# Half sums of the activations at other places in VectorE's order, one of them moved from GpSimd to VectorE

## The chip, the cores and the metric

The kernel runs on one core of a Trainium2 chip. The metric is the device time of one execution in microseconds (us); of several executions the median is given. TensorE does the matrix products, VectorE and ScalarE read their results out of the score banks (PSUM) and work on them, GpSimd takes a share of the elementwise work and issues part of the transfers, and DMA queues move data. An engine executes its instructions in the order of its own queue; engines wait for each other by semaphores.

## The reference

Eight batches of eight heads of attention over 576 positions with 64 features, each head with one of two masks, and then two linear layers with a leaky activation:

```
scores = where(mask, q @ k.T / 8, -1e9)         # heads 0-3: the last 32 positions; heads 4-7: every 32nd
attn   = softmax(scores)
x      = (attn @ v), heads side by side          # 4608 tokens x 512
h      = x @ w_in                                # 512 -> 2048
g      = max(h, 0) + alpha * min(h, 0)
out    = g @ w_out                               # 2048 -> 512
```

## The kernel before

The 4608 tokens are nine chunks of 512 (n = 0 to 8). For each chunk the outer loop runs through positions i. At i = 0 to 15, layer 1 (`lin1_piece`, L608 to L619) makes one 128-row piece of h each: four TensorE products into a bank `hps`, ScalarE's `neg` from the bank (L616), and, one step later, VectorE's `gT` from `neg` and the bank (L619). The bank is free when that `gT` is done; there are three such banks. In chunks 2 to 8 the order of the pieces puts the even ones of each half ahead of the odd ones.

Layer 2 of chunks 2 to 8 (`lin2_fast`, L733 and L743) forms its product from seven block products instead of eight, which takes sums of blocks of g and of w_out. g is cut into token halves t and interleaved feature halves j, g(t, j), and the four sums (here S0 to S3, in the code `gsum[0..3]`, made by `g_sum`, L677) are

- S0 = g(1,0) + g(1,1)
- S1 = S0 - g(0,0)
- S2 = g(0,0) - g(1,0)
- S3 = g(0,1) - S1

Each sum is made in two halves h: half 0 from pieces 0 to 7 (made at i = 0 to 7), half 1 from pieces 8 to 15. A table `sums` says after which position i which half of which sum is made, and on which engine. At i = 16 and 17, TensorE multiplies g(0,0); at 18 it takes S0's half 0 and at 19 S0's half 1 (L733); at 20 and 21 S1's halves; at 22 and 23 g(0,1); at 24 and 25 S2; at 26 and 27 S3; at 28 and 29 g(1,1). The first S0 product takes the bank that the last `gT` has freed.

Between these positions stand the steps of attention for later batches (`attn_n`), in chunks 1 to 6: a head pair's scores on TensorE (L376, banks `sp` and `sph`), their exponentials on ScalarE (L399, L405), the product with a mask on GpSimd (L401, L408), the product with v on TensorE (L429, bank `pv`), and the normalization on VectorE: the reciprocal of the row sum (L436) and the product with it (L438, into `x` or `x16s`). `pv`, `sph` and the transposes `tp` and `xp` share three banks (`pspool`) in turn, so a later one waits until the normalization of an earlier one has read its bank. A strided pair has three such normalizations in a row (`x16s`).

Nothing reorders the instructions: each engine has them in the order in which the loop emits them. At the end of position i the loop first runs the attention steps due there, and then the half sums that the table lists for i.

Of the kernel before, what the change touches and what calls it, by code (L numbers as in the profile page):

```python
# [32 lines left out]
def kernel(  # L33
# [540 lines left out]
    def attn_until(b):  # L574

        return max(i for i, (g, _) in enumerate(pieces) if g == 4 * b + 3) + 1
# [3 lines left out]
    def attn_step(end):  # L580
        while late:
            late.pop(0)()
        if pos["i"] < end:
            pieces[pos["i"]][1]()
            pos["i"] += 1
        if defer:
            defer.pop(0)()
        while after:
            after.pop(0)()
# [6 lines left out]
    def lin1_piece(n, m, begin=False):  # L596
        if n not in gTs:
            gTs[n] = gpool.tile([128, 16, 512], F16, tag="gT", name="gT")
        c0 = (512 * n) % RING
        hps = begun.pop(m, None)  # L600
        if hps is None:
            pool, tag = (pspool, "ps") if n == 0 and m // 3 % 2 else (phpool, "hps")
            hps = pool.tile([128, 512], F32, tag=tag, name="hps")
            order = (2, 3, 0, 1)
        else:
            order = (0, 1)
        for kk in order[0:2] if begin else order:
            keep(nc.tensor.matmul(  # L608
                hps, win16[:, kk, 128 * m : 128 * m + 128], xT[:, kk, c0 : c0 + 512],
                start=(kk == 2), stop=(kk == 1)))  # L610
        if begin:
            begun[m] = hps
            return

        neg = npool.tile([128, 512], F32, tag="neg", name="neg")
        keep(nc.scalar.activation(neg, hps, AF.Relu, scale=-1.0))  # L616

        def fin():
            keep(nc.vector.scalar_tensor_tensor(  # L619
                gTs[n][:, m, :], neg, oma[:, m : m + 1], hps, op0=ALU.mult, op1=ALU.add))  # L620
        late.append(fin)
# [3 lines left out]
    def lin2_piece(n, i):  # L625
        mt, part = i // 4, i % 4
        last = n == NCH - 1
        if part == 0:
            ops_cur["t"] = phpool.tile([128, 512], F32, tag="hps", name="ops")
        ops = ops_cur["t"]  # L630
        r0 = 512 * n + 128 * mt
        if last and mt == 3:

            if part in (1, 3):
                return
            c0 = 128 * part
            half = phpool.tile([128, 512], F32, tag="hps", name="ops3") if part else ops
            for kf in range(16):
                keep(nc.tensor.matmul(
                    half[:, 0:256], gTs[n][:, kf, 128 * mt : 128 * mt + 128],  # L640
                    wout16[:, kf, c0 : c0 + 256], start=(kf == 0), stop=(kf == 15)))
            osb = opool.tile([128, 512], F32, tag="osb", name="osb")
            keep(nc.vector.tensor_copy(osb[:, 0:256], half[:, 0:256]))
            keep(nc.sync.dma_start(out[r0 : r0 + 128, c0 : c0 + 256], osb[:, 0:256]))
            return
        for kf in range(4 * part, 4 * part + 4):
            keep(nc.tensor.matmul(  # L647
                ops, gTs[n][:, kf, 128 * mt : 128 * mt + 128], wout16[:, kf, :],
                start=(kf == 0), stop=(kf == 15)))
        if part == 3:  # L650
            osb = opool.tile([128, 512], F32, tag="osb", name="osb")
            keep(nc.scalar.copy(osb, ops))
            keep(nc.sync.dma_start(out[r0 : r0 + 128, :], osb))


    def wout_sum(i):

        def w(j, c):
            return wout16.rearrange("p (i j) c -> p i j c", j=2)[:, :, j, 256 * c : 256 * c + 256]

        o, a, b = (
            (0, w(0, 1), w(0, 0)), (1, w(1, 1), wsum[0]),
            (2, w(1, 1), w(0, 1)), (3, w(1, 0), wsum[1]))[i]
        keep(nc.vector.tensor_tensor(wsum[o], a, b, op=ALU.subtract))

    def g_sum(n, i, h, eng="dve"):

        gv = gTs[n].rearrange("p (i j) c -> p i j c", j=2)
        hs = slice(4 * h, 4 * h + 4)

        def g(t, j):
            return gv[:, hs, j, 256 * t : 256 * t + 256]

        a, b, op = (
            (g(1, 0), g(1, 1), ALU.add), (gsum[0][:, hs], g(0, 0), ALU.subtract),
            (g(0, 0), g(1, 0), ALU.subtract), (g(0, 1), gsum[1][:, hs], ALU.subtract))[i]
        keep((nc.vector if eng == "dve" else nc.gpsimd).tensor_tensor(gsum[i][:, hs], a, b, op=op))  # L677
# [149 lines left out]
    def attn_n(n, end):  # L827
        for _ in range(n):
            attn_step(end)
        if n == 0:  # L830
            attn_step(0)
# [108 lines left out]
    for pr in range(2):  # L940
# [5 lines left out]

    FAST = 2
    sums = {
        5: [(2, 0, "pool")], 9: [(0, 0, "pool")], 15: [(0, 1, "dve"), (1, 0, "dve")],
        16: [(1, 1, "dve")], 18: [(2, 1, "dve")], 19: [(3, 0, "dve")], 20: [(3, 1, "dve")]}  # L950

    for n in range(1, NCH):
        ab = attn_until(n + 1) if n + 1 < B else len(pieces)
        left = ab - pos["i"]
        acc = -1.5 if n == 1 else 0.0
        for i in range(32 if n < FAST else 30):
            if i < 16:
                lin1_piece(n, i if n < FAST else 8 * (i // 8) + 2 * (i % 4) + i % 8 // 4)
            elif n < FAST:
                lin2_piece(n, i - 16)  # L960
            else:
                lin2_fast(n, i - 16)
            acc += left / (22 if n < FAST else 19.5 if n == B - 2 else 21) * (0.5 if i < 16 else 1.0)
            cnt = int(acc)
            acc -= cnt
            attn_n(cnt, ab)
            if n < FAST:
                if i in (18, 21, 24, 27):
                    wout_sum((i - 18) // 3)
                continue  # L970
            for z, h, eng in sums.get(i, ()):
                g_sum(n, z, h, eng)
        while pos["i"] < ab:
            attn_step(ab)
# [30 lines left out]
```

## Time and profile before

| what | value |
|---|---|
| median of 3 runs | 299.87 us (299.77 to 300.31) |
| profiled execution, time | 300.08 us |
| profiled execution, span of the core | 298.3 us |
| half sums on VectorE (L677) | 42, shortest 0.675 us, longest 1.767 us |
| half sums on GpSimd (L677) | 14, median 2.122 us |
| start of layer 1, chunk by chunk, 3 to 8 | 122.74, 153.05, 183.36, 213.67, 242.69, 268.74 us |

A profile is of one execution. In the rows of a timeline the first number is the start in us from the span's start, the second the length in us, then engine, line, operation, the tiles (written <- read), the shapes, the count of merged instructions, and in brackets the idle time before them with what ended it. "PE" is TensorE, "DVE" VectorE, "ACT" ScalarE, "POOL" GpSimd.

### The profile page before, as it was taken

To read this page: it belongs to the slowest core of one execution; us is meant where nothing else is said; L and a number is where in the kernel's file an instruction comes from. 1 tells how busy PE (TensorE), PEld (TensorE's weight loads), DVE (VectorE), ACT (ScalarE), POOL (GpSimd) and SP (SyncE) were. 2 spreads that over 40 slices of the span, in tenths; PEclk is the share of its full clock that TensorE was granted. 3 is DMA by queue.
4 is the path that set the end of the run, shared out by engine and by line. 5 is a ranking of instruction groups with operands and counts; after the bars stand their busy time and mean duration, and the time that the engine had idled before them with its cause. 6 is when DMAs were issued, how large, how long until landed. Compare 5 with 4: busy or idle time off the path is not lost.

```text
span 298.3 us, 6835 instructions
## 1 busy us (share of the span) xinstructions
PE 292.3 (98%) x2684; PEld 182.7 (61%) x2684; DVE 219.1 (73%) x406; ACT 178.5 (60%) x332; POOL 175.5 (59%) x164
## 2 busy tenths in 40 slices
PE   8999999999999999999999999999999999999995
PEld 3764555544554477646864687468745974784484
DVE  5688876668775897588848984898489948926852
ACT  1777755697557774776477646764676356516730
POOL 8462571059869998979897988495553405002300
PEclk9999999999999999999999999999999999999999
DMA  7999999999998969999999999967711140022004
GB/s 183 256 194 201 242 206 260 206 185 321 126 193 144 115 100 102 206 156 139 123 154 180 156 138 177 174 98 79 211 22 21 20 144 2 0 73 70 0 2 142
DMA packets 96976, 41.18 MB, mean 138 GB/s; under 512 B 75360, under 2 KB 93232, under 8 KB 96944
## 3 DMA queue, kind: packets, MB, share of 16 engines
q0 software_dynamic: 51008, 17.77, 60.8%
q1 hardware_dynamic: 45584, 22.32, 34.7%
q10 hardware_dynamic: 352, 0.66, 0.9%
q8 instruction: 21, 0.34, 0.5%
q14 instruction: 11, 0.09, 0.1%
HBM read 38.24 MB, written 9.44 MB: 160 GB/s over the span
## 4 chain that ended last, share of the span: by engine, by line
PE 80%; DVE 8%; ACT 4%; DMA 3%; issue 3%; SPq 1%; POOL 0%; DVEq 0%; ACTq 0%
PE hps L608 38%; PE ops L743 18%; PE ops L647 5%; PE ops L733 5%; PE pv L429 4%; DMA ql<-in_q_dram 3%; DVE gsum L677 2%; PE ops L908 2%; PE sp L376 2%; DVE gT L619 2%; DVE x16s L438 1%; ACT neg L616 1%; PE sph L376 1%; PE xp L454 1%; DVE x L438 1%
## 5 line engine op out<-in xcount | busy, mean ns | idle before, releaser
L608 PE MATMUL hps<-xT,win 128*128 128x512 f16 x576 | 132.2, 379 | 0.0
L619 DVE SCALAR_TENSOR_TENSOR gT<-neg,oma,hps 128x512 f16<-128x512 f32 x144 | 105.3, 744 | 36.0 <-ACT neg L616 28.1
L616 ACT ACTIVATE neg<-hps 128x512 f32<-128x512 f32 x144 | 85.8, 597 | 34.6 <-PE hps L608 32.5
L608 PEld LDWEIGHTS <-win 128*128 128x128 f16 x576 | 53.5, 98 | 58.6 <-issue 0.2
L677 POOL TENSOR_TENSOR gsum<-gT 128x1024 f16<-128x1024 f16 x14 | 29.7, 2123 | 41.7 <-DVE gT L619 36.7
L401 POOL TENSOR_TENSOR et<-et,consts 128x576 f16<-128x576 f16 (+1 forms) x24 | 35.5, 1477 | 28.0 <-ACT et L399 27.9
L743 PEld LDWEIGHTS <-gT 128*128 128x128 f16 x336 | 31.4, 98 | 5.4 <-issue 0.3
L438 DVE TENSOR_TENSOR x<-pv,rc 96x384 f16<-96x384 f32 (+2 forms) x62 | 33.0, 532 | 2.1
L408 POOL TENSOR_TENSOR et<-et,consts 128x576 f16<-128x576 f16 (+1 forms) x24 | 31.5, 1311 | 0.0
L429 PEld LDWEIGHTS <-et 72*128 72x128 f16 (+1 forms) x448 | 23.4, 98 | 11.4 <-DVE x L438 0.8
L743 PE MATMUL ops<-wout,gT 128*128 128x256 f16 x224 | 27.9, 273 | 0.1
L733 PE MATMUL ops<-wsum,gsum 128*128 128x256 f16 x216 | 26.6, 273 | 0.0
L399 ACT ACTIVATE et<-sp 128x576 f16<-128x576 f32 (+1 forms) x24 | 15.5, 644 | 17.1 <-PE sp L376 17.1
L234 POOL COPY vs<-stv 72x1024 f16<-72x1024 f16 x14 | 15.3, 1104 | 16.5 <-DMA stv<-in_v_dram 16.5
L743 PEld LDWEIGHTS <-gsum 128*128 128x128 f16 x224 | 20.8, 98 | 2.6
L733 PEld LDWEIGHTS <-gsum 128*128 128x128 f16 x224 | 20.8, 97 | 2.7
L436 DVE RECIPROCAL rc<-pv 96x6 f32<-96x6 f32 (+2 forms) x80 | 14.6, 183 | 10.2 <-PE pv L429 10.1
L688 DVE TENSOR_TENSOR osb<-ops,par 128x512 f32<-128x512 f32 (+1 forms) x14 | 9.4, 673 | 15.7 <-PE ops L743 8.2
L405 ACT ACTIVATE et<-sph 128x288 f16<-128x288 f32 (+1 forms) x48 | 18.8, 409 | 0.0
L686 ACT COPY osb<-ops 128x512 f32<-128x512 f32 x14 | 8.2, 586 | 16.8 <-PE ops L743 16.7
L647 PE MATMUL ops<-wout,gT 128*128 128x512 f16 x64 | 16.4, 380 | 0.0
L760 ACT COPY par<-ops 128x512 f32<-128x512 f32 x13 | 7.6, 585 | 14.0 <-PE ops L733 14.0
(111 smaller groups left out, 363.4 us busy)
## 6 DMA issues: line engine op xcount, KB each, us to landing
out_dram<-osb SPq DMA_DIRECT2D x35, 256.0 KB, 4.0
vl<-in_v_dram POOLq DMA_DIRECT2D x6, 384.0 KB, 8.6
win<-in_moe_w_in_dram POOLq DMA_DIRECT2D x4, 512.0 KB, 17.9
wout<-in_moe_w_out_dram POOLq DMA_DIRECT2D x4, 512.0 KB, 16.8
qsd<-in_q_dram POOLq DMA_DIRECT2D x7, 288.0 KB, 6.9
ksd<-in_k_dram POOLq DMA_DIRECT2D x7, 288.0 KB, 7.9
stv<-in_v_dram POOLq DMA_DIRECT2D x7, 288.0 KB, 7.3
ql<-in_q_dram SPq DMA_DIRECT2D x3, 576.0 KB, 7.6
```

The source lines that it names most:

```text
L401: keep(nc.gpsimd.tensor_tensor(mv, mv, m, op=ALU.mult))
L405: keep(nc.scalar.activation(ev[:, n * y : n * y + n], sps[y][0:r, 0:n], AF.Exp, scale=SCALE))
L408: keep(nc.gpsimd.tensor_tensor(mv, mv, m, op=ALU.mult))
L429: keep(nc.tensor.matmul(pv[:, 65 * x : 65 * x + 65], et[0:r, c : c + 128], v16[0:r, 2 * P.pr + hh, t, :] if P.strided else v16[:, 6 * (2 * ...
L438: keep(nc.vector.tensor_tensor(P.x16[0:w, c0 : c0 + 64 * nb].rearrange("r (c e) -> r c e", e=64), pvv[:, :, 0:64], rc[0:w, 0:nb].unsqueeze ...
L608: keep(nc.tensor.matmul(hps, win16[:, kk, 128 * m : 128 * m + 128], xT[:, kk, c0 : c0 + 512], start=(kk == 2), stop=(kk == 1)))
L616: keep(nc.scalar.activation(neg, hps, AF.Relu, scale=-1.0))
L619: keep(nc.vector.scalar_tensor_tensor(gTs[n][:, m, :], neg, oma[:, m : m + 1], hps, op0=ALU.mult, op1=ALU.add))
L647: keep(nc.tensor.matmul(ops, gTs[n][:, kf, 128 * mt : 128 * mt + 128], wout16[:, kf, :], start=(kf == 0), stop=(kf == 15)))
L677: keep((nc.vector if eng == "dve" else nc.gpsimd).tensor_tensor(gsum[i][:, hs], a, b, op=op))
L733: keep(nc.tensor.matmul(o, gsum[i][:, y, 128 * z : 128 * z + 128], wsum[i][:, y, :], start=(x == "5" and y == 0 and (z == 0 or alone)), st ...
L743: keep(nc.tensor.matmul(o, lhs(y), rhs(y), start=(first and y == 0), stop=(y == 7), skip_group_check=True))
```

## The change

The table of half sums is replaced by two, one for chunk 2 (`FAST`) and one for chunks 3 to 8. In chunks 3 to 8, S1 half 0 is made at i = 13 instead of 15, S1 half 1 at 17 instead of 16, S2 half 1 at 19 instead of 18, and S3 half 0 at 20 instead of 19. In chunk 2, S0 half 0 is made by VectorE at i = 12 instead of by GpSimd at i = 9, S1 half 0 stays at 15, and the rest is as in the other table. The work of every half sum is the same.

```diff
     FAST = 2
     sums = {
-        5: [(2, 0, "pool")], 9: [(0, 0, "pool")], 15: [(0, 1, "dve"), (1, 0, "dve")],
-        16: [(1, 1, "dve")], 18: [(2, 1, "dve")], 19: [(3, 0, "dve")], 20: [(3, 1, "dve")]}
+        5: [(2, 0, "pool")], 9: [(0, 0, "pool")], 13: [(1, 0, "dve")], 15: [(0, 1, "dve")],
+        17: [(1, 1, "dve")], 19: [(2, 1, "dve")], 20: [(3, 0, "dve"), (3, 1, "dve")]}
+    sums2 = {
+        5: [(2, 0, "pool")], 12: [(0, 0, "dve")], 15: [(0, 1, "dve"), (1, 0, "dve")],
+        17: [(1, 1, "dve")], 19: [(2, 1, "dve")], 20: [(3, 0, "dve"), (3, 1, "dve")]}
...
-            for z, h, eng in sums.get(i, ()):
+            for z, h, eng in (sums2 if n == FAST else sums).get(i, ()):
                 g_sum(n, z, h, eng)
```

An entry `i: [(z, h, engine)]` reads: after position i, half h of sum Sz on that engine.

## The prediction

> **What bounds the kernel now.** First the page: TensorE is busy 98% of the span at the full granted clock, so only time that TensorE itself loses can be won back.
>
> ```profile
> PE 292.3 (98%) x2684; PEld 182.7 (61%) x2684; DVE 219.1 (73%) x406; ACT 178.5 (60%) x332; POOL 175.5 (59%) x164
> ...
> PEclk9999999999999999999999999999999999999999
> ```
>
> Busy time hides short waits, since a matmul's recorded length covers its successor's start. So I read TensorE's timeline from start to start where the change works: chunk 3 (its second layer starts at 138.07), with chunks 4 and 5 repeating it 30.31 us and 60.62 us later, and chunk 2.
>
> ```profile
> 143.03 0.30 PE L376 MATMUL sp<-qT,kT 64*128 64x96 f16 x6
> 143.16 0.56 PE L376 MATMUL sph<-qT,kT 64*128 64x96 f16 x6
> 143.65 1.05 PE L733 MATMUL ops<-wsum,gsum 128*128 128x256 f16 x8
> 144.66 0.34 PE L429 MATMUL pv<-vs,et 72*128 72x65 f16 x6
> ...
> 149.61 0.30 PE L376 MATMUL sp<-qT,kT 64*128 64x96 f16 x6
> 149.75 0.29 PE L376 MATMUL sph<-qT,kT 64*128 64x96 f16 x6
> 149.97 1.05 PE L743 MATMUL ops<-wout,gsum 128*128 128x256 f16 x8
> 150.86 0.35 PE L429 MATMUL pv<-vl,et 128*128 128x65 f16 x6
> ```
>
> The same scores and product appear twice. The first time, scores take 143.65 - 143.03 = 0.62 us and the product 144.66 - 143.65 = 1.01; the second time 0.36 and 0.89. So TensorE loses 0.26 + 0.12 = 0.38 us. What it waits for is on VectorE:
>
> ```profile
> 136.17 1.39 DVE L619 SCALAR_TENSOR_TENSOR gT<-neg,oma,hps 128x512 f16<-128x512 f32 x2
> 138.04 1.61 DVE L619 SCALAR_TENSOR_TENSOR gT<-neg,oma,hps 128x512 f16<-128x512 f32 x2 [0.48 <-ACT neg L616]
> 139.68 1.10 DVE L677 TENSOR_TENSOR gsum<-gT 128x1024 f16<-128x1024 f16 x1
> 140.71 0.68 DVE L677 TENSOR_TENSOR gsum<-gsum,gT 128x1024 f16<-128x1024 f16 x1
> 141.31 0.18 DVE L436 RECIPROCAL rc<-pv 72x6 f32<-72x6 f32 x1
> 141.52 0.55 DVE L438 TENSOR_TENSOR x16s<-pv,rc 72x384 f16<-72x384 f32 x1
> 141.99 0.68 DVE L677 TENSOR_TENSOR gsum<-gsum,gT 128x1024 f16<-128x1024 f16 x1
> ...
> 142.81 0.55 DVE L438 TENSOR_TENSOR x16s<-pv,rc 72x384 f16<-72x384 f32 x1
> ...
> 144.09 0.42 DVE L438 TENSOR_TENSOR x16s<-pv,rc 72x256 f16<-72x256 f32 x1
> ```
>
> Three normalizations of the strided pair end at 142.07, 143.36 and 144.51. Each frees one of three score banks: the second frees the bank of the second sph (restarted at 143.42), the third that of the pv at 144.66. Ahead of the second stand three half sums, and a fourth ahead of the third. VectorE still had 0.48 us idle inside layer 1. GpSimd's mask products lie beside this:
>
> ```profile
> 137.70 1.29 POOL L401 TENSOR_TENSOR et<-et,consts 72x576 f16<-72x576 f16 x1
> 138.94 1.28 POOL L408 TENSOR_TENSOR et<-et,consts 72x576 f16<-72x576 f16 x1
> ```
>
> The sum at 139.68 needs 1.10 instead of 0.68: it ended 0.56 after the mask product (140.22). Sum and mask product exclude each other. The other way round, a mask product caught behind a sum ends 1.13 after it (chunk 6: sum ends 231.49, product 232.62). VectorE's gT and normalizations (0.74, 0.55) keep their length beside mask products, so only the sums fight.
>
> Chunk 2 loses more:
>
> ```profile
> 110.94 0.67 PE L292 MATMUL tp<-consts,kl 128*128 128x128 f16 x9
> 111.58 1.05 PE L733 MATMUL ops<-wsum,gsum 128*128 128x256 f16 x8
> 112.87 0.30 PE L429 MATMUL pv<-vs,et 72*128 72x65 f16 x4 [0.25 <-DVE x16s L438]
> ```
>
> The transposes to product step is 0.64, and 0.50 at 107.63 where nothing waits: 0.14, for S1 half 0, ended 111.52. The eight matmuls take 1.29, and 0.87 elsewhere: 0.41 (rounded), for the second normalization (ends 112.81). Together 0.55.
>
> **The change, part by part.** The instructions are the same but for one half sum that passes from GpSimd (2.14 us) to VectorE (0.68). No DMA is added; the DMA issues behind GpSimd's moved sum come sooner. In the built order, VectorE has S1 half 0 between the gT of i = 13 and 14, and two normalizations together before S1 half 1.
>
> *Chunks 3 to 5, gain.* With S1 half 0 gone from its old place, the first two normalizations follow S0 half 1 directly. If S0 half 1 ends at 141.08 (below), they end near 141.8 and 142.5, before the second sph's bank is asked for at 143.2; S1 half 1 then ends at 143.1, 0.4 before its matmuls at 143.5; the third normalization ends at 143.6, before its pv at 144.4. Both waits go: 0.38 per chunk.
>
> *Chunks 3 to 5, cost.* S1 half 0 follows the gT that ends at 136.17 + 1.39 = 137.56; neighbours overlap by 0.08, so it runs 137.48 to 138.16. Its input from GpSimd has been ready since 134.11 + 2.12 = 136.23. The next gT waits for ScalarE until 138.04 and starts at 138.08 instead: hidden by the 0.48 idle; without it, 0.6 would fall on the last gT, whose bank TensorE takes at 140.19 (0.55 after that gT's end). But the L401 mask product of 137.70 is caught: it ends 138.16 + 1.13 = 139.29, L408 at 139.24 + 1.28 = 140.52, S0 half 1 at 140.52 + 0.56 = 141.08. TensorE needs that at 140.19 + 8 x 0.109 = 141.06, and starts 0.06 after a sum's end: stall 0.08. Bounds: S1 half 0 takes 0.68, or 1.10 as the caught row does; with 1.10 all shifts by 0.42 and the stall is 0.50; with no clash there is none. I take 0.68, since VectorE starts 0.22 ahead of the mask product. GpSimd's four DMA issues at 140.16 slip 0.3; they feed the next chunk. Net 3 x (0.38 - 0.08) = 0.90.
>
> The row of 1.10 comes first; the Trainium skill differs with itself on it: Advanced Engine Details and Errata (VectorE Performance Modes, Mode Summary) has only two-port VectorE instructions clash with GpSimd, while the GPSIMD Engine Reference (Key points) adds those with two SBUF inputs, as these sums are. By the first there would be no stall at all, and the sum would be 0.24 better; the row agrees with the second.
>
> *Chunk 2.* S0 half 0 goes into VectorE's idle 105.21 to 105.77 (0.56): 105.13 to 105.82, less 0.08 overlap, so the next gT is on time. GpSimd, having issued its DMAs by 105.90, does both mask products by about 108.4, not 110.96. S0 half 1 (108.68) and S1 half 0 then take 0.68 each and end at 109.97 rather than 111.52; the second normalization ends at 110.7. Gain 0.55. Were the mask products still in the way, S1 half 0 would end as now, but the second normalization, no longer behind S1 half 1, would still be done by 112.3, before 112.45: 0.41 is the low end.
>
> *Chunk 6.* TensorE waits once, for the gT of i = 13 (228.69), which stands ahead of the moved sum. S0 half 1 then ends at 231.3 against a need at 232.0. Nothing either way.
>
> *Chunks 7 and 8* have no attention to free. The last gT comes every 0.86 us with 0.12 idle each; S1 half 0 (0.68) after the gT ending 256.36 gives 256.97, 257.62, 258.28 against 258.09 now. TensorE takes that gT's bank at 258.26: 0.07 lost (0 to 0.19), in each chunk: 0.14.
>
> **Sum.** 0.55 + 0.90 - 0.14 = 1.31 us. The profiled execution took 300.08 with a span of 298.3 (1.8 around it); it becomes 298.77. The median lies 0.21 below the profiled one: 298.56, so 298.6.
>
> **Rivals.** (a) *GpSimd gets the port first in chunks 3 to 5.* If L401 holds it when S1 half 0 comes, that ends at 138.99 + 0.56 = 139.55, the two gT at 140.20 and 140.86, and TensorE, wanting the bank at 140.19, loses 0.72. Against the 0.38 won: +0.34 x 3 = 1.02, + 0.14 - 0.55 = 0.61 slower, 300.5. It decides once the mask product is ahead by more than today's 0.22 gap. For it: the gap is small. Against: both engines' place follows TensorE's pace, and at 144.16 a mask product begun 0.27 before two sums was still the one held (2.68 instead of 1.28). 13%.
> (b) *The wait moves.* If the caught row's 1.10 applies, or the freed 0.26 reappears at the next bank because the third normalization stays where it is, chunks 3 to 5 give between nothing and a loss of 0.50 - 0.38 = 0.12 each: -0.55 + 0.14 + (0 to 0.36) = -0.41 to -0.05, 299.5 to 299.8. For it: three banks only, and sums that fill every hole of VectorE. Against: the walk leaves 0.7 at the third normalization. 17%.
> (c) *The change does not take effect*: excluded for the order itself, which is as told.
>
> **Numbers.** Forecast 70%, its own range 298.1 (no stall anywhere, 298.2, and scatter) to 299.1 (half of the 0.42 shift in chunks 3 to 5). Leaving out (a), the range is 298.0 to 299.9. A change of 0.2% (0.6 us) is about what can be told from none: faster 70%, same 17% (b), slower 13% (a).
>
> **What would show it.** In chunk 3 the scores step back to 0.36 and the product to 0.89; a step of about 0.08 between the eighth and ninth matmul after 140.19; S0 half 1 about 1.4 long; the L401 mask product near 1.6. In chunk 2 the sums 0.68 each and no wait at the pv. In chunks 7 and 8 0.07 ahead of the first S0 matmul. Wrong if S1 half 0 takes over 1 us in chunks 3 to 5, or if the matmuls of S0's bank wait there.

## The result, and the profile after

The changed kernel takes 309.45 us (median of 6 runs, 307.8 to 311.7) against 299.98 us (299.77 to 300.31): a ratio of 1.0312, 95% interval 1.0286 to 1.0338. It is slower by 9.5 us. The profiled execution took 309.46 us with a span of 307.6.

From the starts of layer 1 in the timelines of both profiles:

| stretch | before, us | after, us | difference |
|---|---|---|---|
| up to chunk 2 | 91.25 | 91.41 | +0.16 |
| chunk 2 | 31.49 | 35.10 | +3.61 |
| chunks 3, 4, 5, each | 30.31 | 31.89 | +1.58 (4.74 in all) |
| chunk 6 | 29.02 | 29.03 | +0.01 |
| chunk 7 | 26.05 | 26.11 | +0.06 |
| chunk 8, to the end of the last matmul | 26.32 | 26.40 | +0.08 |
| from there to the end of the span | 3.20 | 3.92 | +0.72 |

The busy times and the clock on the page after:

```profile
PE 293.4 (95%) x2684; PEld 184.4 (60%) x2684; DVE 226.3 (74%) x407; ACT 178.5 (58%) x332; POOL 170.9 (56%) x163
...
PEclk9999999999999979999999999999999999999999
```

TensorE's busy share falls from 98% to 95%, and one slice of the clock shows 7 instead of 9. Who makes it wait stands in the view of waits, of TensorE alone (total us, times, longest):

```profile
PE ops L733 <- DVE gT L619: 5.4, 3, 1.8
PE ops L743 <- DVE gT L619: 2.7, 1, 2.7
```

Three waits ahead of L733, the first S0 product of chunks 3, 4 and 5, and one ahead of L743, the start of layer 2 in chunk 2. All wait for a late `gT`. VectorE in chunk 3 after:

```profile
139.94 1.39 DVE L619 SCALAR_TENSOR_TENSOR gT<-neg,oma,hps 128x512 f16<-128x512 f32 x2
141.25 3.29 DVE L677 TENSOR_TENSOR gsum<-gsum,gT 128x1024 f16<-128x1024 f16 x1
144.47 1.39 DVE L619 SCALAR_TENSOR_TENSOR gT<-neg,oma,hps 128x512 f16<-128x512 f32 x2
145.90 0.69 DVE L677 TENSOR_TENSOR gsum<-gT 128x1024 f16<-128x1024 f16 x1
```

GpSimd in the same stretch:

```profile
140.73 0.72 POOL L135 DMA_DIRECT2D ksd<-in_k_dram  x1
141.47 1.29 POOL L401 TENSOR_TENSOR et<-et,consts 72x576 f16<-72x576 f16 x1
142.70 1.28 POOL L408 TENSOR_TENSOR et<-et,consts 72x576 f16<-72x576 f16 x1
```

And the exponentials on ScalarE that L401 multiplies; they are done at 140.33 + 0.64 = 140.97, while GpSimd still issues the ksd DMA:

```profile
140.33 0.64 ACT L399 ACTIVATE et<-sp 72x576 f16<-72x576 f32 x1
```

S1 half 0 stands where the prediction put it, and begins 0.22 us before the mask product, as predicted. But it takes 3.29 us instead of 0.68: it ends (144.55) 0.56 after the *second* mask product (143.99). The two last `gT` come behind it, and with them S0's bank. TensorE in chunk 3 after:

```profile
143.77 0.35 PE L429 MATMUL pv<-vs,et 72*128 72x65 f16 x6
145.91 1.91 PE L733 MATMUL ops<-wsum,gsum 128*128 128x256 f16 x16 [1.80 <-DVE gT L619]
...
148.75 0.30 PE L376 MATMUL sp<-qT,kT 64*128 64x96 f16 x6
148.89 0.29 PE L376 MATMUL sph<-qT,kT 64*128 64x96 f16 x6
149.11 1.05 PE L733 MATMUL ops<-wsum,gsum 128*128 128x256 f16 x8
150.00 0.35 PE L429 MATMUL pv<-vs,et 72*128 72x65 f16 x6
```

Both waits that were to go did go: scores to product is 149.11 - 148.75 = 0.36, and the product takes 150.00 - 149.11 = 0.89, as in the undisturbed place of before. From start to start TensorE lost 1.96 at 145.91 (4.08 behind the start of layer 2, against 2.12 before); less the 0.38 won, that is the 1.58 of the table. Chunk 2 has the same on VectorE, with S0 half 0:

```profile
105.29 3.83 DVE L677 TENSOR_TENSOR gsum<-gT 128x1024 f16<-128x1024 f16 x1
```

In chunk 2 TensorE then stood idle for 2.75 us (107.08 to 109.83), and ran at half speed for some time. The windows (PE, PEld, DVE, ACT and POOL busy us with counts, granted clock, DMA share, GB/s):

```profile
105.00:109.00 4.00, 2.08 (x15) 0.96 (x14) 4.00 (x2) 1.68 (x5) 3.99 (x5) 1.00 0.68 105
109.00:112.40 3.40, 2.57 (x17) 2.07 (x17) 3.33 (x7) 0.73 (x2) 2.47 (x4) 0.51 1.41 133
112.40:118.00 5.60, 5.60 (x74) 4.94 (x71) 3.66 (x9) 3.69 (x7) 0.00 (x0) 0.99 0.24 15
```

By these windows the granted clock was one half for about 3.4 us: it fell shortly before the matmuls resumed at 109.83 and was whole again at about 112.4.

### The profile page after: what moved, and what is told of

Read it like the earlier page. It is cut to its first block, busy times and chain, and to the rows that moved or that the text cites. A ratio compares the mean times of both kernels' runs of the same rounds, so it can differ in the third digit from the quotient of the medians.

```text
span 307.6 us, 6835 instructions
## 1 busy us (share of the span) xinstructions
PE 293.4 (95%) x2684; PEld 184.4 (60%) x2684; DVE 226.3 (74%) x407; ACT 178.5 (58%) x332; POOL 170.9 (56%) x163
## 4 chain that ended last, share of the span: by engine, by line
PE 78%; DVE 13%; DMA 3%; ACT 3%; issue 2%; ACTq 0%; DVEq 0%
PE hps L608 29%; PE ops L743 19%; PE ops L733 8%; DVE gT L619 6%; PE ops L647 5%; DVE gsum L677 4%; PE pv L429 3%; PE ops L908 3%; DMA xT<-x 3%; DVE x L438 3%; PE wps L785 3%; ACT neg L616 2%; PE sp L376 2%; PE xp L454 1%; PE ops L923 1%
## 5 line engine op out<-in xcount | busy, mean ns | idle before, releaser
L401 POOL TENSOR_TENSOR et<-et,consts 128x576 f16<-128x576 f16 (+1 forms) x24 | 33.7, 1406 | 41.2 <-ACT et L399 40.9
L677 POOL TENSOR_TENSOR gsum<-gT 128x1024 f16<-128x1024 f16 x13 | 27.6, 2121 | 41.9 <-DVE gT L619 36.9
L743 PEld LDWEIGHTS <-gT 128*128 128x128 f16 x336 | 31.9, 99 | 8.6 <-issue 3.4
L733 PE MATMUL ops<-wsum,gsum 128*128 128x256 f16 x216 | 26.5, 272 | 5.4 <-DVE gT L619 5.4
L743 PE MATMUL ops<-wout,gT 128*128 128x256 f16 x224 | 28.7, 278 | 2.8 <-DVE gT L619 2.7
L408 POOL TENSOR_TENSOR et<-et,consts 128x576 f16<-128x576 f16 (+1 forms) x24 | 31.0, 1291 | 0.0
L733 PEld LDWEIGHTS <-gsum 128*128 128x128 f16 x224 | 21.0, 97 | 8.4 <-issue 5.7
L743 PEld LDWEIGHTS <-gsum 128*128 128x128 f16 x224 | 20.9, 98 | 2.6
L677 DVE TENSOR_TENSOR gsum<-gsum,gT 128x1024 f16<-128x1024 f16 x14 | 17.7, 1263 | 0.1
```

What stands on the lines that cost most here:

```text
L401: keep(nc.gpsimd.tensor_tensor(mv, mv, m, op=ALU.mult))
L408: keep(nc.gpsimd.tensor_tensor(mv, mv, m, op=ALU.mult))
L733: keep(nc.tensor.matmul(o, gsum[i][:, y, 128 * z : 128 * z + 128], wsum[i][:, y, :], start=(x == "5" and y == 0 and (z == 0 or alone)), st ...
L743: keep(nc.tensor.matmul(o, lhs(y), rhs(y), start=(first and y == 0), stop=(y == 7), skip_group_check=True))
```

## The experiments

The tables are those of the diff above, written in short; `t2`, `t35` and `t68` are those of chunk 2, chunks 3 to 5 and chunks 6 to 8. "The port" is a name for what lets only one of a VectorE sum and a GpSimd product work at a time, as the rows show it. Theory A: GpSimd keeps the port for a mask product from the moment its input is ready. Theory B: the issue of the qsd and ksd DMAs holds it. Theory C: the sum waits for data.

**The two places apart.** First chunk 2 alone, then chunks 3 to 8 alone:

```diff
 t2 : 5: (2,0) pool   12: (0,0) dve   15: (0,1) (1,0)   17: (1,1)   19: (2,1)   20: (3,0) (3,1)
-t35, t68 : as changed
+t35, t68 : as before
```

> Chunk 2's table as changed, chunks 3 to 8 as before. If the two losses are local and add up, chunk 2 is about 3.6 us longer than before (S0 half 0 held for 3.8 us, and TensorE at half clock behind its stall), chunks 3 to 5 stay at 30.3: about 303.6. Rival: the losses of chunks 3 to 5 follow from chunk 2's shift of GpSimd's queue; then they stay at 31.9 here, and the time is near the changed kernel's 309.

303.92 us (ratio 1.0135, interval 1.0096 to 1.0174); chunks 3 to 5 are back at 30.32, chunk 2 is 33.84 in its profile.

> Chunk 2 as before, chunks 3 to 8 as changed. Local losses: 1.58 us in each of chunks 3 to 5 and 0.07 in 7 and 8, 4.9 in all: about 304.8, at the full clock throughout. Rival (it follows from chunk 2): near 300.

304.92 us (1.0177, 1.015 to 1.0204): chunk 2 at 31.48, chunks 3 to 5 at 31.89. The two losses are local and separate: 3.9 and 4.9 us in the medians, of 9.5 together. In the profile of chunk 2 alone the same idle 2.75 us was followed by no half clock:

```profile
109.42 1.03 PE L743 MATMUL ops<-wout,gT 128*128 128x256 f16 x8 [2.75 <-DVE gT L619]
```

The same eight matmuls took 1.87 us in the changed kernel. So chunk 2's +3.61 divides into 33.84 - 31.49 = 2.35 for the stall less the gain, and 35.10 - 33.84 = 1.26 for the clock. The four runs of this kernel fall into two pairs: 302.86 and 302.93 at a mean clock of 1.0 and 0.997, 304.91 and 305.09 at 0.994. The changed kernel's six runs spread in the same way: 307.8 and 308.6 at 0.999, 309.44 to 309.88 at 0.992 to 0.994, 311.7 at 0.986. So 7.8 to 8.6 of its 9.5 us are there without the lower clock.

**No mask products.** The changed kernel leaves out both mask products of each head pair; its attention is unmasked.

```diff
-                keep(nc.gpsimd.tensor_tensor(mv, mv, m, op=ALU.mult))
...
-                if y:
-                    keep(nc.gpsimd.tensor_tensor(mv, mv, m, op=ALU.mult))
```

> The changed kernel with the two mask products of each head pair left out from batch 2 on (attention there is unmasked). Theory A, the port is kept by mask products: S1 half 0 of chunk 3 takes 0.68 and S0 half 0 of chunk 2 0.69, no stall ahead of S0's bank, though the qsd and ksd DMAs are still issued beside them. Theory B, these DMA issues hold the port: both sums are still held until the ksd issue ends, 0.9 to 1.3 us long. Theory C, the sums wait for their data: 3.3 and 3.8 as in the changed kernel.

S1 half 0 of chunk 3 takes 0.68, S0 half 0 of chunk 2 0.77, and no stall stands ahead of S0's bank. So the sums had not waited for their data: C falls. But without mask products GpSimd had issued qsd and ksd long before, and it was the issue of kr that ran beside the sum:

```profile
140.71 0.68 DVE L674 TENSOR_TENSOR gsum<-gsum,gT 128x1024 f16<-128x1024 f16 x1
```

```profile
138.03 0.72 POOL L135 DMA_DIRECT2D ksd<-in_k_dram  x1
138.74 2.94 POOL L116 DMA_DIRECT2D kr<-in_k_dram  x4
141.64 2.06 POOL L234 COPY vs<-stv 72x1024 f16<-72x1024 f16 x2
```

So it leaves B open. A copy on GpSimd holds a sum as well: S0 half 1 (142.91) takes 1.34 there and ends 0.55 after the copies above. (Its time, 303.52 in one run, holds other waits: TensorE waits 1.34 and 0.46 us for ScalarE's copies at chunk 2's start, and from 94.16 to 97.58 the clock is one half.)

**The sum 0.66 us sooner.**

```diff
 t2, t68 : as before
-t35 : 13: (1,0) dve
+t35 : 12: (1,0) dve
```

> Before, with chunks 3 to 5 as changed but S1 half 0 after i = 12 instead of 13, so 0.66 us sooner: it is asked for at 136.82 of the old clock, after the qsd issue has begun and before ScalarE has finished the exponentials (137.20) that the first mask product needs. Theory A (mask products keep the port once they are ready to run): the sum takes 0.68, all three waits of chunks 3 to 5 go, 0.38 each: 1.1 faster, 298.8. Theory B (the DMA issue holds the port): the sum is held to the end of the second mask product as before, at least 1.6 slower per chunk, 304.8 or more.

299.34 us against 299.89 (0.9981, 0.9971 to 0.9991); chunks 3 to 5 at 30.08. VectorE, then GpSimd, in chunk 3:

```profile
136.81 0.68 DVE L677 TENSOR_TENSOR gsum<-gsum,gT 128x1024 f16<-128x1024 f16 x1
```

```profile
136.16 0.79 POOL L135 DMA_DIRECT2D qsd<-in_q_dram  x1
136.95 0.72 POOL L135 DMA_DIRECT2D ksd<-in_k_dram  x1
137.68 1.28 POOL L401 TENSOR_TENSOR et<-et,consts 72x576 f16<-72x576 f16 x1
```

ScalarE's exponentials for L401:

```profile
136.55 0.64 ACT L399 ACTIVATE et<-sp 72x576 f16<-72x576 f32 x1
```

The sum runs beside both issues at full speed: B falls. The gain is 0.23 per chunk rather than 0.38, since the next `gT` is later and TensorE waits 0.15 for its bank at the start of layer 2.

**The sum in its changed place, but the mask products ready later.**

```diff
+                if P.hp == 3 and 4 <= P.b <= 6:
+                    keep(nc.scalar.copy(idle[:, 0:576], consts[:, 0:576]))
                 keep(nc.scalar.activation(
```

> Before, with chunks 3 to 5 as changed (S1 half 0 after i = 13), and one more ScalarE copy (128x576, its result unused, some 0.5 to 0.7 us) ahead of the exponentials that the held sum's mask products wait for. They then end near 137.8 of the old clock, and the sum is asked for at 137.48, ahead of them. Theory A (a mask product keeps the port from the moment its input is ready, even behind unfinished DMA issues): the sum takes 0.68 in chunks 3 to 5. Rival (what decides is that the sum starts beside the ksd issue, with a mask product next in the queue): it still takes 3.3.

The sum takes 0.68 in all three chunks, beside the same issue of ksd and directly ahead of the mask product. It is now the mask product that is caught (1.46). In this kernel the lines are numbered up to three higher:

```profile
137.63 0.68 DVE L680 TENSOR_TENSOR gsum<-gsum,gT 128x1024 f16<-128x1024 f16 x1
```

```profile
137.12 0.72 POOL L136 DMA_DIRECT2D ksd<-in_k_dram  x1
138.00 1.46 POOL L404 TENSOR_TENSOR et<-et,consts 72x576 f16<-72x576 f16 x1 [0.15 <-ACT et L402]
```

```profile
137.27 0.65 ACT L402 ACTIVATE et<-sp 72x576 f16<-72x576 f32 x1
```

So the rival named there falls, and A is borne out at this place. Chunks 3 and 5 take 30.02 and 30.03, which is 0.29 less than before. Chunk 4 takes 30.30: its mask products were caught for longer and S0 half 1 came 0.33 late. Chunk 6 is 0.28 longer than before, by a later `gT` at the start of its layer 2; the one run took 300.12 us.

**The sum 0.66 us later**, while the first mask product runs:

```diff
-t35 : 13: (1,0) dve
+t35 : 14: (1,0) dve
```

> Before, with chunks 3 to 5 as changed but S1 half 0 after i = 14, so that it is asked for at 138.75 of the old clock, while the first mask product runs. If the sum and the mask products take turns, as in chunk 2 of before, it ends 0.56 after the first mask product (about 0.8 long) and the last gT 0.6 late: S0's bank costs 0.06 and S0 half 1 0.1 to 0.2, against the 0.38 won, so 0.1 to 0.2 faster per chunk: about 299.4. If a sum always waits for both mask products, it is 2.0 long and chunks 3 to 5 are 0.9 longer each: about 302.6.

302.75 us (1.0086, 1.0072 to 1.0101); chunks 3 to 5 at 31.25, 0.94 longer. The second of the two cases:

```profile
138.71 2.09 DVE L677 TENSOR_TENSOR gsum<-gsum,gT 128x1024 f16<-128x1024 f16 x1
```

```profile
137.72 1.29 POOL L401 TENSOR_TENSOR et<-et,consts 72x576 f16<-72x576 f16 x1
138.96 1.28 POOL L408 TENSOR_TENSOR et<-et,consts 72x576 f16<-72x576 f16 x1
```

The sum sits out both mask products (it ends at 140.80, 0.56 after the second).

**What is left of the change without sums inside layer 1.** Against the kernel before:

```diff
 t2, t35, t68 : 5: (2,0) pool   9: (0,0) pool   15: (0,1) (1,0)
-t2, t35, t68 : 16: (1,1)   18: (2,1)   19: (3,0)   20: (3,1)
+t2, t35, t68 : 17: (1,1)   19: (2,1)   20: (3,0) (3,1)
```

> The changed kernel with S0 half 0 of chunk 2 on GpSimd after i = 9 and S1 half 0 of all chunks after i = 15 again, behind S0 half 1; what is left of the change is that S1 half 1, S2 and S3 stand behind the normalizations. No sum is asked for inside layer 1. Chunks 3 to 5 lose both waits, 0.36 each, chunk 2 0.4 of its 0.55: 1.5 faster, 298.4. Rival (the wait moves to the third normalization): 0.24 each and 0.4, 298.8.

298.66 us (298.59 to 298.76), a ratio of 0.995 (0.9938 to 0.9961): faster than both kernels. Chunks 3 to 5 take 29.96, 0.35 less than before; chunk 2 takes 31.33, so 0.16 instead of the 0.4 expected: TensorE now waits 0.29 there for S1 half 1, which stands behind the second normalization.

The same with S1 half 0 after i = 12 in chunks 3 to 5:

> As the run with S1 half 0 after i = 15 everywhere, but after i = 12 in chunks 3 to 5, where it took 0.68 and cost 0.15 ahead of layer 2: 0.23 each and 0.4 in chunk 2, 1.1 faster, 298.8.

299.32 us (0.9969, 0.9957 to 0.9981): the 0.15 ahead of layer 2 is paid again, chunks 3 to 5 at 30.08.

**The same for chunk 2**, the sum on VectorE but sooner:

```diff
-t2 : 12: (0,0) dve
+t2 : 11: (0,0) dve
 t35, t68 : as before
```

> Before, with chunk 2's table as changed but S0 half 0 after i = 11 instead of 12: it is asked for at about 104.3 of the old clock, while GpSimd still makes S2 half 0 (ends 104.43), and the first mask product becomes ready only with the end of its exponentials at 104.96. Theory A: the sum is held by GpSimd's sum alone, ends 0.56 after it, near 105.0, some 0.7 long; the next gT is 0.4 late and caught up in the idle time before the one after; chunk 2 has both its gains: 0.55 shorter, 299.4. Rival (a sum that comes upon GpSimd at work waits until both mask products are through): 4 us long, TensorE stalls for 2.5 to 3 us as in the changed kernel, 302 to 304.

S0 half 0 starts at 104.21, directly behind GpSimd's own sum, and takes 0.68; the exponentials end at 104.85. Chunk 2 takes 30.93, 0.56 less than before. Yet the time is 300.26 against 300.19 (1.0006, 0.9997 to 1.0015): the profile has lost it again behind the last matmul, as the next run shows.

Both together:

> Chunks 3 to 8 as in the run with S1 half 0 after i = 15 everywhere, chunk 2 with S0 half 0 on VectorE after i = 11. Theory A: 0.55 instead of 0.16 won in chunk 2: 298.3. Rival: 301 to 303.

299.16 us (0.9974, 0.9964 to 0.9984), 0.5 *above* the run that leaves chunk 2's sum on GpSimd, though its chunk 2 is 0.40 shorter. VectorE's last add, in that run and in this one:

```profile
293.84 0.42 DVE L688 TENSOR_TENSOR osb<-opsl,par 128x256 f32<-128x256 f32 x1 [2.38 <-PE opsl L743]
```

```profile
293.92 0.42 DVE L688 TENSOR_TENSOR osb<-opsl,par 128x256 f32<-128x256 f32 x1 [2.73 <-PE opsl L743]
```

The last matmul ends at 293.75 and 293.47: the add follows after 0.09 in the one and after 0.45 in the other, and the rest of the span is 3.2 and 4.0 us. All five profiles with chunk 2's sum on VectorE up to here have it at 0.45, all others at 0.09. These programs have one more instruction on VectorE, so two kernels changed the count elsewhere. First, two more:

```diff
+    keep(nc.vector.memset(kTs[0][:, :, 0:32], 0.0))
+    keep(nc.vector.memset(kTs[0][:, :, 608:672], 0.0))
```

> The run with S1 half 0 after i = 15 everywhere, and two of VectorE's small memsets at the program's start made twice. If the late last add (0.45 instead of 0.09 after TensorE's last matmul) comes with the count of instructions on VectorE, it is late here too, the part after the last matmul is 3.9 instead of 3.2, and the time 0.7 above that run: 299.4. Rival (it comes with the half sum moved in chunk 2): 0.09, and 298.7.

299.74 us, 1.1 above the run without the two. The add is at 0.09 here, against what was expected, but VectorE's next instruction (the program's closing one) at 0.49 instead of 0.14, and the rest of the span is 4.08. Then two fewer, with chunk 2's sum on VectorE:

```diff
-    keep(nc.vector.memset(kTs[0][:, :, 0:32], 0.0))
-    keep(nc.vector.memset(kTs[0][:, :, 608:672], 0.0))
+    keep(nc.gpsimd.memset(kTs[0][:, :, 0:32], 0.0))
+    keep(nc.gpsimd.memset(kTs[0][:, :, 608:672], 0.0))
```

> The run with S0 half 0 on VectorE after i = 11 and S1 half 0 after i = 15, with the same two memsets on GpSimd instead. By the count of instructions: the last add at 0.09, 298.3, below every run so far. Rival: late as before, 299.2.

298.57 us (298.38 to 298.57; 0.9948, 0.9933 to 0.9962), the add at 0.09, the rest 3.19. So the late end comes without the moved sum and stays away with it: in these profiles it goes with the count of VectorE's instructions. These last two kernels are one case each, and the second also gives GpSimd two more.

## Why the prediction was wrong

*Which waits bound TensorE, and what they were worth: right.* The scores and the product in chunks 3 to 5 won their 0.38 (stall 1.96 less 1.58), and chunk 2 won 0.56 where 0.55 was predicted, as soon as its sum was free (30.93 against 31.49).

*Where the sums would stand and what follows: right.* S1 half 0 began 0.22 ahead of the mask product; chunk 6 changed by 0.01; chunks 7 and 8 lost 0.06 and 0.08 where 0.07 was predicted.

*The step that failed* is the length of the moved sums: "S1 half 0 takes 0.68, or 1.10 as the caught row does ... I take 0.68, since VectorE starts 0.22 ahead of the mask product." It took 3.29 in chunks 3 to 5, and S0 half 0, which was to run 105.13 to 105.82, took 3.83. For chunk 2 no clash of this sum was considered at all. The bound of 1.10 came from a sum that met the *second* mask product with nothing behind it. The rule by which I chose, who starts first, is not the one that decides. In order of time, from the timelines:

| run, chunk | exponentials of the mask product's input end | sum starts | mask product starts | sum takes |
|---|---|---|---|---|
| changed, 2 | 105.12 | 105.29 | 106.05 | 3.83 |
| changed, 3 | 140.96 | 141.25 | 141.47 | 3.29 |
| S1 half 0 after i = 14, 3 | 137.21 | 138.71 | 137.72 | 2.09 |
| copy ahead of the exponentials, 3 | 137.91 | 137.63 | 138.00 | 0.68 |
| copy ahead of the exponentials, 4 | 167.94 | 167.94 | 168.03 | 0.68 |
| S1 half 0 after i = 12, 3 | 137.18 | 136.81 | 137.68 | 0.68 |
| S0 half 0 after i = 11, 2 | 104.85 | 104.21 | 105.77 | 0.68 |

In these rows a sum that starts 0.17 us or more after the input is ready is held, even if GpSimd still issues DMAs for 0.76 us; one that starts no later than the input is ready is not, even 0.09 us ahead of the mask product. So at these places GpSimd acts as if its claim began with its input's readiness, not with its own start. The claim itself is not seen in a trace. Nor do the rows force this reading: those with the copy are the only ones in which GpSimd stood idle ahead of the mask product (0.15 us), and without them the lead of the sum over the mask product would divide the rows as well (held at 0.76 us and less, free at 0.87 and more). And the held sums waited for both mask products.

It is no rule for every place. The prediction's own counterexample, in chunk 3 of the kernel before, goes against it:

```profile
143.43 0.65 ACT L399 ACTIVATE et<-sp 128x576 f16<-128x576 f32 x1 [0.71 <-PE sp L376]
144.16 2.68 POOL L401 TENSOR_TENSOR et<-et,consts 128x576 f16<-128x576 f16 x1 [1.04 <-ACT et L399]
144.43 1.28 DVE L677 TENSOR_TENSOR gsum<-gT,gsum 128x1024 f16<-128x1024 f16 x2
```

Here the input is ready at 144.08 and the mask product has started at 144.16, yet two sums from 144.43 take 0.68 each and the mask product is held; chunks 4 and 5 repeat it. GpSimd had stood idle for 1.04 us there, while in all the held rows of the table it came straight from issuing a DMA. Whether that is what makes the difference was not tested.

*Rival (a)* had the mechanism, GpSimd first, but with a wrong point of decision (the 0.22 between the starts, instead of the exponentials) and a wrong price (0.72 of stall for one mask product, instead of 1.96 for two). Its argument against, that both engines keep their distance, was true and beside the point: at that distance the sum was held. My other argument, the mask product of 144.16 that two sums held up, is a true case of the opposite outcome, but it did not carry over.

*What no term had:* the clock, 1.26 of chunk 2's loss in this profile, which fell behind the long stall in some executions and not in others; and the 0.72 behind the last matmul, which comes with one more instruction on VectorE.

What stays open: why GpSimd went first at the changed places and the sums at 144.43. And in chunk 2 of the kernel before, a sum that started (108.68) while the first mask product ran got its turn ahead of the second; the sum after i = 14 did not. What decides was found in neither case.

## What to carry to other kernels

Before an elementwise operation with two SBUF inputs is moved on VectorE, look at when the inputs of GpSimd's next operations become ready, and not only at when these start: a GpSimd operation that waits behind its own queue can already keep the sum out, and the price can be the whole run of such operations. Place the sum ahead of that moment or behind the run, and read its length in a trace. A hidden gap of VectorE is worth nothing if the port is not free in it.

## What the runs showed of the hardware that was not expected

- A sum can be held by GpSimd operations that start after it, as in the table (0.22 us after it in chunk 3, 0.76 in chunk 2), and a mask product by sums that start 0.27 after it. The Trainium skill (GPSIMD Engine Reference, Key points) tells of contention with VectorE instructions that have two SBUF inputs, and the traces agree (0.68 against 1.10 to 3.83).
- After 2.75 us without a matmul the clock was halved for 3.4 us in one profile and not in another of the same stall (matmuls of 1.87 against 1.03 for eight). The Trainium skill (TensorE: Matmul & The Clock Gate, What's actually happening) names an idle window of about 3.4 us that runs freely; the length of the slow stretch agrees, while here a shorter idle time was enough. In the kernel without mask products the clock fell to one half (94.16) shortly behind idle times of 1.34 and 0.46 us.
- The six profiles with one or two more instructions on VectorE than the kernel before have 3.9 to 4.1 us behind TensorE's last matmul; the other eight have 3.2 to 3.4. The cause was not sought further.
